# First batch of a spectral mixer: how its 64-point transforms are loaded, laid out and transposed

## The chip, the cores and the metric

The kernel runs on one core of one Trainium2 chip. The metric is the device time of one execution in microseconds, as the median of several runs. A profile of one execution goes with it: the start, the length and the waits of every instruction on each engine of the core.

The engines are named as the profile names them: PE is TensorE's matmul and PEld its weight load, DVE is VectorE, ACT is ScalarE, POOL is GpSimd, SP is SyncE, which here only issues DMAs.

## The reference

The input x has 8 batches of 3008 rows and 256 channels, all fp32. Two steps are computed.

1. A global filter: a real Fourier transform along the 3008 rows, a product with a complex filter, and the inverse transform.
2. An MLP-mixer layer on the result y: a token MLP across the rows (3008 to 256, ReLU, 256 to 3008) with a residual, then a channel MLP (256 to 1536, ReLU, 1536 to 256) with a residual.

```python
y = irfft(rfft(x, axis=1) * (filt_r + 1j * filt_i), n=3008, axis=1)
h = np.maximum(y.transpose(0, 2, 1) @ w_tok1, 0.0) @ w_tok2
u = y + h.transpose(0, 2, 1)
out = u + np.maximum(u @ w_ch1, 0.0) @ w_ch2
```

The mixer's weights arrive as 8-byte floating-point numbers; the kernel turns them into fp32 on the chip.

## The kernel before

**The transform.** 3008 is 47 x 64. The kernel does the transform of 3008 in two stages: first transforms of length 64 (over n2), with rows n1 and 47 - n1 laid together in one tile of 128 partitions, and then transforms of length 47 (over n1), one for each of 32 frequencies k2. Between them the data have to change places: what was a row index in the free dimension has to become a partition. For the batches after the first this goes through DRAM (`z_tmp`). For the first batch, which nothing can overlap with, it is done on the chip by DVE's transposition of 32 x 32 blocks.

**The first batch, step by step.** The constants at the top are A = 24 (rows n1 in a half), XC = 2, NXC = 12, K2 = 32, D = 256, P = 128 and HALF = 64.

- `x_load` (L486) loads one of 12 units. For batch 0 a unit is 4 rows n1 and 128 of the 256 channels (`xc, dc = 2 * XC, D // 2`, L489): units 0 to 5 hold the left half of the channels, 6 to 11 the right half. A piece that lies together in DRAM is 128 fp32 (512 bytes). The lower 64 partitions are loaded by SP, the upper 64 by POOL. The last unit of each half has a missing row and takes two small DMAs more on POOL (L512 and L513).
- `a_unit` (L528) is a matmul of the unit (128 x 512) with the table `wa0`, and for batch 0 a copy by ACT (L533) into the buffer `turned`. Two PSUM banks are used in turn.
- `turned` (L211 to L213) is [128, 32, 256], with the row index s (24 used, 8 zeroed by a memset at L1235) outside and the channel d inside. Its tile also holds `wa0` at its end.
- After unit 5 and again after unit 11, DVE turns the channels that are complete, 16 at a time (L617 to L621). Each of the 16 instructions takes 16 channels x 32 rows s in place, with a step of 256 fp32 between successive s.
- `b_unit(k)` (L640), for the 32 values of k, is a matmul (L642) whose moving operand is `turned[:, k, :]`, 256 fp32 that lie together, and a product with the filter on DVE (L647). `bi_unit(k)` (L650) is the inverse of that stage: four matmuls (L656), a copy on ACT (L666) and, for each pair of k, a store to `g_tmp`.

**What lies beside it.** While `b_unit` and `bi_unit` run, the same loop (L1240 to L1269) turns the token MLP's weights into fp32 in 16 steps, one for each pair of k: loads by SP or POOL, ACT L276, DVE L278 to L284, PE L322 and L323, ACT L325. The filter of each pair of k is loaded by POOL (`filt_load`, L236 to L243), copied to the upper partitions by ACT (`filt_double`, L248), and its table is turned by ACT (L255 and L256).

**The order of the work.** The schedule is manual: instructions are issued on each engine in the order in which the program text produces them. The generator `dft(GROUPS[0])` gives up control after each unit, and the loop at L1240 places other work there. At `i == NXC - 1`, which is after the last unit and before the second group of transpositions, it issues on ACT the copies of the first weight tiles (`copies()`) and the loads of four constants of 128 x 128 (L1251): `wa`, `was`, `wai` and `ident`. `ident` is used by the last six of the weight conversions on PE, the others from the second batch's transform and the first mixing step on.

**After the first batch** the result is read back from `g_tmp` (L778), the token sums run on PE (L784), and then the mixer runs through 8 batches of 6 blocks of rows and 6 blocks of channels, with the transforms of the following batches set between its steps. This takes the rest of the time.

Of the kernel before, what the change touches and what calls it, by code (L numbers as in the profile page):

```python
# [10 lines left out]
FP32 = mybir.dt.float32  # L11
# [11 lines left out]
D = 256  # L23
P = 128
K2 = 32
A = 24
KR = 4 * A
KH = KR // 2
HALF = 64
XC = 2  # L30
NXC = A // XC
# [5 lines left out]
WC = 2  # L37
# [14 lines left out]
AP = A // 2  # L52
W1S = 7
IN_B = 16
EARLY = 12
GROUPS = ((0,), (1, 2), (3, 4), (5, 6), (7,))

# [70 lines left out]
def kernel(  # L128
# [11 lines left out]
    nc = tc.nc  # L140
# [69 lines left out]

    turned = wcp.tile([P, K2 * D + P], FP32, tag="wc", name="turned")  # L211
    wa0 = turned[:, K2 * D:]
    turned = turned[:, 0:K2 * D].rearrange("p (s d) -> p s d", d=D)  # L213
    chan = []


# [233 lines left out]
    def copies():  # L450

        while copied[0] < len(tiles) and copied[0] <= ended[0] + 1:
            advance(copy)
            copied[0] += 1
# [34 lines left out]
    def x_load(b, c, i, queue=None):  # L489

        where, tag = ((t3p, "t3"), (tp, "t"), (vp, "v"), (up, "u"), (t1p, "t1"), (t2p, "t2"), (wbp, "wb"))[c // 2 if b == 0 else 6]
        xc, dc = (2 * XC, D // 2) if b == 0 else (XC, D)
        d0, c = divmod(c, A // xc)
        j = i - XB
        if b and j >= 0:
            j %= XF
            t = filts[j // 2][:, j % 2]
        else:
            t = where.tile([P, xc, dc], FP32, tag=tag, name="x")

        def rows(n1, ap):
            xb = x[b]
            return bass.AP(tensor=xb.tensor, offset=xb.offset + n1 * D + d0 * dc, ap=ap + [[1, dc]])

        for h in range(2):
            n = xc - 1 if h and (c + 1) * xc == A else xc
            q = queue or (nc.gpsimd if b == 0 and h else nc.sync)
            q.dma_start(t[h * HALF:(h + 1) * HALF, 0:n, :],
                        rows(A + c * xc if h else A - 1 - c * xc, [[N1 * D, N2], [D if h else -D, n]]))
            if n < xc:  # L510

                q.dma_start(t[HALF:P - 1, n, :], rows(N1, [[N1 * D, N2 - 1]]))  # L512
                q.dma_start(t[P - 1:P, n, :], rows(0, [[N1 * D, 1]]))  # L513
        xs[b, c + d0 * (A // xc)] = t

    def rows_of(t_d, b):
        g, i = place_of[b]
# [10 lines left out]
    def a_unit(b, c):  # L528
        ps = bank(free_bank())
        nc.tensor.matmul(ps, wa0 if b == 0 else wa, xs.pop((b, c)).rearrange("p a d -> p (a d)"), start=True, stop=True)  # L530
        if b == 0:
            d0, c = divmod(c, NXC // 2)
            nc.scalar.copy(out=turned[:, ts(c, 2 * XC), ds(d0 * P, P)], in_=ps.rearrange("p (a d) -> p a d", d=P))  # L533
            return
        z_out(b, ps, c, nc.scalar)

# [20 lines left out]
    def dft(bs):  # L557
# [44 lines left out]
        for i, u in enumerate(todo):  # L602
            if tiled:
                now, sd = sd, x_sums(*todo[i + 1], i + 1) if i + 1 < len(todo) else None
                more(1)
                a_pair(*u, now)
                yield "a" if i + 1 < len(todo) else "w"
                continue
            if first and i in (0, 2):
                w_load(i // 2)  # L610
            if first and i in (6, 8):
                table_load(i // 2 - 1)
            a_unit(*u)
            if bs != GROUPS[1] or i >= XB:
                more(1)
            yield "a" if i + 1 < len(todo) else "w"
            if first and (i + 1) % (NXC // 2) == 0:  # L617

                for d in range(i // (NXC // 2) * P, (i + 1) // (NXC // 2) * P, 16):
                    v = turned.rearrange("p s d -> p d s")[:, d:d + 16, :]  # L620
                    nc.vector.transpose(v, v)  # L621
        t2s, t3s, prods = {}, {}, {}
        wide = per * nb

# [14 lines left out]

        def b_unit(k):  # L640
            ps = bank("pg").rearrange("p (b d) -> p b d", b=2)[:, 0:nb, :]
            nc.tensor.matmul(ps, wbs[k // WC][:, 0:2 * P:2, k % WC], turned[:, k, :].unsqueeze(1), start=True, stop=True)  # L642
            t = filts_0[k // KC % len(filts_0)]
            if k == 0:
                prods["all"] = p1p.tile([P, 2, 2, D], FP32, tag="p1", name="p1")
            p1 = prods["all"][:, k % 2]
            nc.vector.tensor_tensor(out=p1, in0=ps.to_broadcast([P, 2, D]), in1=t[:, :, k % KC, :], op=ALU.mult)  # L647
            prods[k] = (p1[:, 0:1], p1[:, 1:2])
# [583 lines left out]

    with tc.manual_schedule():
        nc.sync.dma_start(wa0, wa0_d)
        nc.vector.memset(turned[:, A:K2, :], 0.0)  # L1235
        for t in filts:
            nc.vector.memset(t, 0.0)
        half = 0
        second = dft(GROUPS[1])
        for i, _ in enumerate(dft(GROUPS[0])):  # L1240
            if i == 0:
                nc.scalar.dma_start(wai_t, wait_d)
            k = i - NXC - 2

            if i < NXC:
                if i in (1, 3, 5, 7, 9):
                    start()
                if i == NXC - 1:
                    copies()
                    for t, src in ((wa, wa_d), (was, was_d), (wai, wai_d), (ident, ident_d)):  # L1250
                        nc.scalar.dma_start(t, src)  # L1251
            elif k >= 0:
                if k == K2 - 5:
                    pause.append(True)
                while half < 2 * IN_B * (k + 1) // K2:
                    if half % 2:
                        convert_end()
                    else:
                        convert_middle()
                    half += 1  # L1260

                if 19 <= k < 25:
                    t4_load(0, k - 19, 0, PARTS[1])
                elif 26 <= k < 29:
                    for c in range(2):
                        t4_load(0, 2 * (k - 26) + c, PARTS[1], PARTS[2])
                elif k in (30, 31):
                    for c in range(3):
                        t4_load(0, 3 * (k - 30) + c, PARTS[2], PARTS[3])  # L1269
        pause.clear()  # L1270

        fill(5)
        for c in range(A // TC4):
            t4_load(0, c, PARTS[3], P, (nc.sync, nc.gpsimd)[c % 2])
        both = wcp.tile([P, 2, JP, 7, P], FP32, tag="wc", name="wc")

        chan.extend((both[:, 0], both[:, 1]))
        next(second)
        for i in range(IN_B, A // 2 + TC * W2G):
            convert()  # L1280
            if i == A // 2 + BY_PE - 1:
                sum_up()
                acc = token_sums(0)

        ahead[0](XF, nc.gpsimd)
        h1s[0] = token_relu(0, acc)
        for dh in range(DH):
            convert()
            u_part(0, 0, dh)
        for f in v_steps(0, 0):  # L1290
            f()
        convert_end(False)
        for _ in range(XB):
            next(second)
        group, todo, done = -1, iter(()), True

        def next_ready(b):
            return done or b != GROUPS[group][-1]

        coming = "a"
        n = MT * JP
        for b, i, place in mix(next_ready):
            if group + 1 < len(GROUPS) and b == GROUPS[group + 1][0]:
                if not done:
                    raise AssertionError("the filter's steps don't fit beside the mixer's")
                group += 1
                done = group + 1 == len(GROUPS)
                todo = iter(()) if done else dft(GROUPS[group + 1]) if group else second  # L1310
                coming = "a"
            if done:
                continue
            jp = i % JP
            if coming in "aw":
                due = place == 1 or (place != 1.5 if group == 0 else coming == "w")
            elif group:
                tail = i >= n - JP
                due = (jp, place) in {"b": ((1, 1.5), (3 if tail else 4, 1.5)), "m": ((2, 2) if tail else (3, 1), (5, 1)),
                                      "i": ((0, 1.5), (3 if tail else 4, 1.5))}[coming]  # L1320
            else:
                due = (jp - (coming == "i")) % JP in ((5, 1, 2, 3) if i < 4 * JP else (5, 0, 1, 2, 3)) and place == {"b": 1, "m": 2, "i": 0}[coming]
            if coming == "a" and group == 0 and i < JP - 1:
                due = {0: 2, 1: 0, 1.5: 0, 2: 1}[place]
            for _ in range(due):
                if not done:
                    coming = next(todo, "end")
                    done = coming == "end"
# [30 lines left out]
```

## Time and profile before

| What | Value |
|---|---|
| Time, median of 3 runs | 2419.13 us (2417.92 to 2422.47) |
| The profiled execution's own time | 2419.85 us |
| Span of its instructions | 2418.1 us |
| PE busy | 2378.0 us, 98% of the span |
| DVE busy | 1940.6 us, 80% |
| First L642 matmul | 31.44 us after the span's start |
| First token-sum matmul (L784) | 111.56 us |
| Mean granted TensorE clock | 0.995 of full speed |

A row of a group of instructions reads: line, engine, operation, output and inputs by their names in the program, shapes, count, then busy time in us and the mean length of one in ns, and then the idle time of the engine just before them with what ended it. A row in order of time begins with start and length in us. Where several instructions are merged into one row (x16), the length is that of the whole group. The length of one instruction is longer than the distance from one start to the next, because instructions of an engine overlap a little.

### The profile page before, as it was taken

To read this page: it belongs to the slowest core of one execution; us is meant where nothing else is said; L and a number is where in the kernel's file an instruction comes from. 1 tells how busy PE (TensorE), PEld (TensorE's weight loads), DVE (VectorE), ACT (ScalarE), POOL (GpSimd) and SP (SyncE) were. 2 spreads that over 40 slices of the span, in tenths; PEclk is the share of its full clock that TensorE was granted. 3 is DMA by queue.
4 is the path that set the end of the run, shared out by engine and by line. 5 is a ranking of instruction groups with operands and counts; after the bars stand their busy time and mean duration, and the time that the engine had idled before them with its cause. 6 is when DMAs were issued, how large, how long until landed. Compare 5 with 4: busy or idle time off the path is not lost.

```text
span 2418.1 us, 35463 instructions
## 1 busy us (share of the span) xinstructions
PE 2378.0 (98%) x12340; PEld 1987.3 (82%) x12340; DVE 1940.6 (80%) x3673; ACT 685.9 (28%) x1339; POOL 619.8 (26%) x1115
## 2 busy tenths in 40 slices
PE   7999999999999999999999999999999999999998
PEld 4666676978888888987888888897888988898887
DVE  7798778787887888777888888877888777777776
ACT  5733322232221222123222222313222222222222
POOL 7476332113111211211121112112212112112121
PEclk8999999999999999999999999999999999999999
DMA  9985546554343232545344223434434111311100
GB/s 211 254 233 168 156 143 177 158 158 135 111 132 95 79 89 72 168 125 156 101 121 136 79 78 86 123 122 127 125 109 143 58 60 36 115 63 31 40 14 21
DMA packets 186011, 278.65 MB, mean 115 GB/s; under 512 B 35101, under 2 KB 122859, under 8 KB 185832
## 3 DMA queue, kind: packets, MB, share of 16 engines
q1 hardware_dynamic: 139544, 212.56, 29.3%
q0 software_dynamic: 34688, 53.83, 8.4%
q10 hardware_dynamic: 11600, 10.00, 1.3%
q8 instruction: 98, 1.61, 0.3%
q14 instruction: 81, 0.66, 0.1%
HBM read 193.52 MB, written 82.72 MB: 114 GB/s over the span
## 4 chain that ended last, share of the span: by engine, by line
PE 88%; DVE 6%; DMA 3%; issue 1%; ACT 1%; SPq 0%; POOL 0%; DVEq 0%; ACTq 0%; POOLq 0%
PE ps_po L1003 33%; PE ps_pg L969 18%; PE ps_pg L985 14%; PE ps_b L523 4%; PE ps_b L835 3%; PE ps_acc L890 3%; PE ps_acc L835 2%; PE ps_b L890 2%; PE ps_b L868 2%; PE ps_acc L868 2%; PE ps_pg L523 1%; DVE t L947 1%; DMA filt<-in_x_dram 1%; PE ps_b L784 1%; DVE hh L947 1%
## 5 line engine op out<-in xcount | busy, mean ns | idle before, releaser
L1011 POOL DMA_DIRECT2D out_dram<-r x752 | 408.7, 552 | 1539.2 <-issue 933.8
L990 ACT ACTIVATE hh<-hh 128x512 f32<-128x512 f32 (+1 forms) x576 | 347.7, 621 | 994.3 <-DVE hh L947 985.7
L947 DVE TENSOR_TENSOR hh<-ps_pg,s 128x512 f32<-128x512 f32 (+3 forms) x864 | 481.8, 585 | 178.8 <-ACT s L972 176.6
L1003 PE MATMUL ps_po<-t,wc 128*128 128x256 f32 (+1 forms) x2296 | 549.6, 379 | 1.8 <-DVE t L947 1.8
L1003 PEld LDWEIGHTS ps_po<-t,wc 128*128 128x128 f32 x2296 | 427.1, 190 | 119.7 <-issue 37.7
L969 PE MATMUL ps_pg<-v,wc 128*128 128x256 f32 (+1 forms) x1728 | 414.4, 376 | 0.1
L1003 PE MATMUL ps_po<-hh,wc 128*128 128x256 f32 (+1 forms) x1722 | 412.0, 375 | 0.7 <-POOL wc L382 0.7
L969 PEld LDWEIGHTS ps_pg<-v,wc 128*128 128x128 f32 x1728 | 328.1, 190 | 40.5 <-DVE v L947 3.2
L1003 PEld LDWEIGHTS ps_po<-hh,wc 128*128 128x128 f32 x1722 | 326.9, 190 | 39.3 <-POOL wc L382 1.9
L985 PE MATMUL ps_pg<-u,wc 128*128 128x256 f32 (+1 forms) x1152 | 292.9, 377 | 1.3 <-DVE hh L947 1.3
L947 DVE TENSOR_TENSOR t<-t,hh 128x256 f32<-128x256 f32 (+1 forms) x576 | 245.5, 426 | 19.8
L985 PEld LDWEIGHTS ps_pg<-u,wc 128*128 128x128 f32 x1152 | 216.8, 190 | 44.3 <-DVE hh L947 13.8
L947 DVE TENSOR_TENSOR s<-ps_pg,hh 128x512 f32<-128x512 f32 (+1 forms) x288 | 196.0, 681 | 30.3 <-DVE hh L947 0.5
L972 ACT COPY s<-ps_pg 128x256 f32<-128x256 f32 (+1 forms) x288 | 106.0, 368 | 350.8 <-PE ps_pg L969 348.6
L947 DVE TENSOR_TENSOR t<-hh 128x512 f32<-128x512 f32 (+1 forms) x288 | 195.3, 678 | 0.6 <-ACT hh L990 0.6
L969 PE MATMUL ps_pg<-u,wc 128*128 128x256 f32 (+1 forms) x576 | 169.6, 376 | 2.5 <-DVE hh L947 2.5
L985 PE MATMUL ps_pg<-v,wc 128*128 128x256 f32 (+1 forms) x576 | 168.7, 375 | 0.0
L947 DVE TENSOR_TENSOR u<-ps_acc,u 128x256 f32<-128x256 f32 (+1 forms) x84 | 46.2, 550 | 97.4 <-PE ps_acc L890 66.7
L969 PEld LDWEIGHTS ps_pg<-u,wc 128*128 128x128 f32 x576 | 108.1, 190 | 18.8 <-DVE hh L947 5.7
L985 PEld LDWEIGHTS ps_pg<-v,wc 128*128 128x128 f32 x576 | 109.1, 190 | 12.6
L947 DVE TENSOR_TENSOR u<-ps_b,u 128x512 f32<-128x512 f32 (+2 forms) x126 | 74.5, 591 | 28.9 <-PE ps_b L890 26.7
L890 PE MATMUL ps_acc<-w 128*128 128x256 f32 (+1 forms) x336 | 85.5, 377 | 1.0 <-ACT t L539 1.0
(161 smaller groups left out, 2655.3 us busy)
## 6 DMA issues: line engine op xcount, KB each, us to landing
w<-w_tmp SPq DMA_DIRECT2D x84, 448.0 KB
w<-w_tmp SPq DMA_DIRECT2D x35, 896.0 KB
out_dram<-r POOLq DMA_DIRECT2D x696, 32.0 KB, 2.9
g_tmp<-t SPq DMA_DIRECT2D x112, 192.0 KB
t<-g_tmp SPq DMA_DIRECT2D x42, 512.0 KB
t<-z_tmp SPq DMA_DIRECT2D x180, 96.0 KB
z_tmp<-t SPq DMA_DIRECT2D x60, 256.0 KB
filt<-in_x_dram SPq DMA_DIRECT2D x90, 128.0 KB
```

The lines of the kernel that those rows point to most:

```text
L523: nc.tensor.matmul(outs(i, j), stat(i, j), mov(i, j), start=True, stop=True)
L784: nc.tensor.matmul(acc[:, t, :], w1[:, a, ts(t, P)], t4[b, a // TC4][:, a % TC4, :], start=(a == 0 and t == 0), stop=(a == A - 1 and t == ...
L835: nc.tensor.matmul(ps[:, at], w[:, n], mov, start=(j == 0 and i in (0, 2)), stop=(j == AP - 1 and i >= 5))
L868: nc.tensor.matmul(ps[:, ds(q * P, n)], t4[b, c][:, r, ts(dh, P)], wai[:, 0:n], start=(first and q == 0), stop=(not first and q == 3))
L890: nc.tensor.matmul(ps[:, ds(j * hw, hw)], h1[:, n, :], w2m[m % 2][:, at, 0:hw], start=(i < 2 and j == 0), stop=(j == len(todo) - 1))
L947: nc.vector.tensor_tensor(out=out, in0=in0, in1=in1, op=op)
L969: nc.tensor.matmul(ps[:, 0:hw], chan[0][:, jp, n, :], mov, start=True, stop=True)
L972: nc.scalar.copy(out=s[:, 0], in_=g[0][:, 0, 0:hw])
L985: nc.tensor.matmul(ps[:, 0:hw], chan[0][:, jp, n, :], mov, start=True, stop=True)
L990: nc.scalar.activation(out=hs, in_=hs, func=AF.Relu)
L1003: nc.tensor.matmul(po[i][:, j, 0:hw], chan[1][:, jp, n, :], mov, start=(jp == 0 and first == 1), stop=(jp == JP - 1 and last == 1))
L1011: q.dma_start(bass.AP(tensor=ob.tensor, offset=ob.offset + row * D + g * cw, ap=[[N1 * D, 32], [D if h else -D, n], [1, cw]]), blocks[ts(g ...
```

## The change

It has four parts, all in the first batch's path.

1. A unit is now 2 rows n1 and all 256 channels, so that a piece that lies together in DRAM is 256 fp32 (1 KB). There are still 12 units, with one missing row in all, so the small POOL DMAs come once and not twice.
2. `turned` is laid out as [128, 64, 32, 4]: the channel d is split into q (64) and r (4), and the row index s stands between them. Successive s are 4 fp32 (16 bytes) apart, and successive q are 128 fp32 apart. ACT's copy writes runs of 8 fp32 from runs of 4 in PSUM. The moving operand of `b_unit` is 64 runs of 4 fp32.
3. All 16 transpositions come after the last unit. Each takes 16 values of q, the 32 rows s and one value of r.
4. The loads of the four constants go from ACT, where they stood ahead of the first filter copy, to SP at the fifth step of the next stage (k == 4).

```diff
+TR = 4
-    turned = turned[:, 0:K2 * D].rearrange("p (s d) -> p s d", d=D)
+    turned = turned[:, 0:K2 * D].rearrange("p (q s r) -> p q s r", s=K2, r=TR)
...
-        xc, dc = (2 * XC, D // 2) if b == 0 else (XC, D)
-        d0, c = divmod(c, A // xc)
+        xc = XC
...
-            t = where.tile([P, xc, dc], FP32, tag=tag, name="x")
+            t = where.tile([P, xc, D], FP32, tag=tag, name="x")
...
         if b == 0:
-            d0, c = divmod(c, NXC // 2)
-            nc.scalar.copy(out=turned[:, ts(c, 2 * XC), ds(d0 * P, P)], in_=ps.rearrange("p (a d) -> p a d", d=P))
+            nc.scalar.copy(out=turned[:, :, ts(c, XC), :], in_=ps.rearrange("p (a q r) -> p q a r", q=D // TR, r=TR))
...
-            if first and (i + 1) % (NXC // 2) == 0:
-
-                for d in range(i // (NXC // 2) * P, (i + 1) // (NXC // 2) * P, 16):
-                    v = turned.rearrange("p s d -> p d s")[:, d:d + 16, :]
-                    nc.vector.transpose(v, v)
+            if first and i + 1 == NXC:
+                for d in range(0, D, HALF):
+                    for r in range(TR):
+                        v = turned[:, d // TR:(d + HALF) // TR, :, r]
+                        nc.vector.transpose(v, v)
...
-            nc.tensor.matmul(ps, wbs[k // WC][:, 0:2 * P:2, k % WC], turned[:, k, :].unsqueeze(1), start=True, stop=True)
+            nc.tensor.matmul(ps.rearrange("p b (q r) -> p (b q) r", r=TR), wbs[k // WC][:, 0:2 * P:2, k % WC],
+                             turned[:, :, k, :], start=True, stop=True)
...
-        nc.vector.memset(turned[:, A:K2, :], 0.0)
+        nc.vector.memset(turned[:, :, A:K2, :], 0.0)
...
                 if i == NXC - 1:
                     copies()
+            elif k >= 0:
+                if k == 4:
                     for t, src in ((wa, wa_d), (was, was_d), (wai, wai_d), (ident, ident_d)):
-                        nc.scalar.dma_start(t, src)
-            elif k >= 0:
+                        nc.sync.dma_start(t, src)
```

More of the change, by code (lines that the diff above doesn't have):

```diff
@@ L498, in x_load @@
         else:
-            t = where.tile([P, xc, dc], FP32, tag=tag, name="x")
+            t = where.tile([P, xc, D], FP32, tag=tag, name="x")
         def rows(n1, ap):
             xb = x[b]
-            return bass.AP(tensor=xb.tensor, offset=xb.offset + n1 * D + d0 * dc, ap=ap + [[1, dc]])
+            return bass.AP(tensor=xb.tensor, offset=xb.offset + n1 * D, ap=ap + [[1, D]])
         for h in range(2):
@@ L513, in x_load @@
                 q.dma_start(t[P - 1:P, n, :], rows(0, [[N1 * D, 1]]))
-        xs[b, c + d0 * (A // xc)] = t
+        xs[b, c] = t
     def rows_of(t_d, b):
```

## The prediction

> **What bounds the kernel now.** I read the page first, then the order of time from 0 to 250 us, then a table of windows, last the groups with shapes kept apart.
>
> ```profile
> span 2418.1 us, 35463 instructions
> PE 2378.0 (98%) x12340; PEld 1987.3 (82%) x12340; DVE 1940.6 (80%) x3673; ACT 685.9 (28%) x1339; POOL 619.8 (26%) x1115
> ```
>
> TensorE (PE) is busy for 98% of the span. The edit leaves the number of its matmuls alone, so the question is when PE can start its long run. The order of time, cut to the lines that matter (start, length, engine, line, what, and in brackets the idle time before and what ended it):
>
> ```profile
> 20.10 1.10 PE L530 MATMUL ps_acc<-x,turned 128*128 128x512 f32 x2 [1.39 <-DMA x<-in_x_dram]
> 21.24 0.59 ACT L533 COPY turned<-ps_acc 128x512 f32<-128x512 f32 x1 [1.90 <-PE ps_acc L530]
> 14.15 17.19 DVE L621 STREAM_TRANSPOSE turned<-turned 128x512 f32<-128x512 f32 x16 [7.94 <-ACT turned L533]
> 26.93 0.68 ACT L276 ACTIVATE both<-st 128x512 f32<-128x512 f32 x1 [4.53 <-DMA st<-in_moe_w_tok_dram]
> 29.09 1.05 ACT L248 COPY filt<-filt 64x1024 f32<-64x1024 f32 x1 [1.48 <-DMA filt<-in_filt_r_dram]
> 31.44 2.07 PE L642 MATMUL ps_pg<-turned,wb 128*128 128x256 f32 x4 [10.24 <-issue]
> ```
>
> The twelfth length-64 unit is transformed at 20.10 us and copied out by 21.83 us. VectorE (DVE) transposes without a gap from 14.15 to 31.34 us: eight transpositions run while the second half of the units is still loading, eight more behind them. PE then starts the next stage (L642) 0.1 us later. The profile calls that wait "issue", but the end of the DVE row gives it away. Is PE the limit from there on?
>
> ```profile
> 2.00:20.00 18.00, 13.27 (x22) 4.25 (x22) 9.58 (x10) 6.46 (x12) 12.98 (x25) 1.00 1.07 228
> 31.40:39.30 7.90, 7.86 (x19) 5.08 (x20) 5.08 (x9) 3.44 (x6) 6.91 (x14) 0.63 1.06 216
> 39.30:56.70 17.40, 17.40 (x65) 13.11 (x64) 13.14 (x24) 14.94 (x27) 13.26 (x25) 1.00 0.91 227
> 56.70:74.10 17.40, 17.40 (x65) 13.12 (x64) 13.29 (x24) 15.54 (x28) 12.52 (x23) 1.00 0.98 248
> 74.10:91.50 17.40, 17.40 (x65) 13.16 (x64) 13.05 (x25) 15.49 (x29) 12.17 (x22) 1.00 0.92 232
> ```
>
> Columns: window, PE, PEld, DVE, ACT, POOL busy with counts, clock, DMA share, GB/s. In three windows of four pairs each PE is busy for all 17.40 us with the same 65 matmuls: 4.35 us a pair. So PE limits this stage, and a later start moves it as a whole. From 91.5 to 188 us the limit passes to the copies on ACT and DVE, the reload of g, the token sums on PE and DVE's conversions. All of them follow the stage in program order, so a delay passes through at a factor of about 1. The price of the change is thus the new time of L642's start less 31.44 us.
>
> [...]
>
> ```profile
> L621 DVE STREAM_TRANSPOSE turned<-turned 128x512 f32<-128x512 f32 x16 | 17.2, 1158 | 7.9 <-ACT turned L533 7.9
> L1082 DVE STREAM_TRANSPOSE r<-u 128x512 f32<-128x512 f32 x80 | 52.3, 686 | 0.0
> L255 ACT COPY turn_i<-wb 64x192 f32<-64x192 f32 x16 | 8.6, 539 | 0.4
> L248 ACT COPY filt<-filt 64x1024 f32<-64x1024 f32 x16 | 16.7, 1044 | 1.8 <-DMA filt<-in_filt_r_dram 1.5
> L656 PEld LDWEIGHTS ps_b<-p,wb 128*96 128x96 f32 x32 | 7.6, 261 | 1.0 <-DVE p L647 0.9
> L656 PEld LDWEIGHTS ps_b<-p,turn_i 128*96 128x96 f32 x32 | 5.5, 170 | 1.0
> ```
>
> A transposition of the same 128x512 takes 686 ns from dense rows (L1082) and 1158 ns at steps of 1 KB (L621; 17.19/16 = 1.074 us start to start). ACT reads at 16-byte steps in L255: 192 elements in 539 ns. The L248 and L990 rows (1024 elements 1044 ns, 512 elements 630 ns) give 0.81 ns an element and 216 ns fixed; so L255 pays (539-216)/192 = 1.68 ns, twice the dense price. PE's weight load pays 261 ns for 96 columns at 16-byte steps against 170 dense. [...] L1082 against L1051 (128 elements, 278 ns) gives (686-278)/384 = 1.06 ns an element, L621 about twice that. [...]
>
> **The change part by part.** *Loads of whole rows.* The same 3.08 MB in half as many packets, and POOL issues two fewer DMAs before the last unit (one L512 and L513 pair, 0.58 + 0.54 us). The x data take 3.08 MB / 228 GB/s = 13.5 us of a saturated queue; [...] Bounds: 0 (other loads take the room) and 3.5 (3.08 MB at the 271 GB/s of the window from 24 to 26 us, 11.4 us, and the issues on top). I take 2.0.
>
> *Copies into the new layout.* Twelve copies of 586 ns; PSUM is now read, and SBUF written, in 16- and 32-byte pieces. Bounds 0.54 (a little quicker) and 1.1 us (double). Only the last one lies on the path; I take 0.6, no difference. The first memset (1.76 us, done at 3.0) has four microseconds of cover; doubled it would still end before the first copy at 7.25, having pushed the three filter memsets to 8 us.
>
> *Transpositions.* Still 16 of 128x512. Their elements stand 16 bytes apart instead of 1 KB[...]. Bounds: 0.60 us (dense, 686 ns less the 0.08 us by which L621's length exceeds its spacing) and 1.2; I take 1.074. All now wait for the last copy, so the eight that had run beside the loads (8 x 1.074 = 8.6 us) come onto the path. Before, 0.9 us of them lay on it already: the second eight were ready at 21.83 but started at 22.74.
>
> *Sum at L642.* Last copy at 21.83 - 2.0 = 19.83; plus 16 x 1.074 = 17.19 and 0.05 hand-over: 37.07 us, against 31.34. Delay 5.7 us.
>
> *Moving operand of L642.* 32 units x 2 matmuls now read runs of four fp32. [...] I take 0. Bounds: 0 (it already runs at 0.215 us for 256 columns, the dense pace) and one extra column time for each run, 0.215/4 = 0.054 us x 64 = +3.4 us in a stage where PE is the limit.
>
> *Constants.* Four ACT issues (0.34 + 0.44 + 0.44 + 0.45 us, 26.96 to 28.74) vanish ahead of L248. ACT ends that work at 31.27 now and would at about 29.5; DVE ends at 37, so it is worth 0. On SP four issues of about 0.4 us stand between a pair of table loads and the token-weight load that follows at the fifth unit of the stage. SP issues some 2.5 us per 4.35-us pair, so 1.85 us is free each pair and the 1.7 us fits; both loads run pairs ahead. Without that cover it would cost 1.7 us once. The constants are needed from 89.95 us (ident) and 140 us (wa) on. The 256 KB are moved, not saved.
>
> Sum against the profiled execution (2419.85 us, span 2418.1): 2419.85 + 5.7 = 2425.6. That execution is 0.72 above the median of 2419.13, so the median becomes **2424.8 us**, 0.24% slower. About 0.2% (4.84 us) is what a measurement of this kernel tells from no change.
>
> **Rivals.**
> 1. *Not slower: the step of 16 bytes is fast on DVE.* Speaking for it: no DVE instruction of before has that step; the 1 KB step might be the special one. Against: ACT and PE pay double at 16 bytes. Price: 16 x 0.60 = 9.6, L642 at 19.83 + 9.65 = 29.5, next late is ACT at 29.5; 1.9 us earlier: 2417.2. It decides below (31.34 - 19.83)/16 = 0.72 us a transposition.
> 2. *The load hides more of it:* x 3.5 us earlier, plus 0.6 us of the 2.1 us that PE waits for the reload of g at 109.4: 5.73 - 1.5 - 0.6 = 3.6, 2422.7. For: that wait is a DMA's, and the queues get ahead while DVE transposes. Against: the g reload follows the stage's own writes.
> 3. *PE pays for the short runs:* 5.7 + 3.4: 2428.2. [...]
>
> **Chances.** Forecast 0.61 (own range 2423.3 to 2426.8, as x gains 3.5 to 0), rival 1 0.14, rival 2 0.13, rival 3 0.10, something else 0.02. Of the forecast some 0.52 lies above 2423.97 (0.2%); with rival 3 and the rest 0.64 slower. Same: 0.09 + 0.13 + most of rival 1 = 0.33. Faster by 4.84 us needs L642 at 26.6, that is 0.42 us a transposition, below the dense row: 0.03. The range takes the forecast's own, rival 2, most of rival 3 and the upper edge of rival 1: 2418.0 to 2429.0, leaving out about 0.17.
>
> **What would show it.** L621's successor: 16 back to back, spacing near 1.07 us, starting near 19.9; L642's first near 37.1; pairs still 4.35 us; the first matmul of the token sums near 117.2 (111.56 now); the last L530 near 18. Wrong if the spacing is under 0.8 us, if pairs stretch, or if the shift at L642 isn't found again at 188 us.

## The result, and the profile after

The changed kernel takes 2428.75 us in the median of 8 runs (2424.63 to 2430.24), against 2421.12 us (2417.92 to 2422.47, 8 runs) of the kernel before beside it. The ratio is 1.0034, with a 95% interval of 1.0025 to 1.0043: 0.34% slower, 6 to 10 us. The prediction had the sign, but 0.24%: 2424.8 us against a median of 2419.13, or 5.7 us. The profiled execution took 2429.18 us. Its page begins:

```profile
span 2427.4 us, 35461 instructions
PE 2378.4 (98%) x12340; PEld 1990.0 (82%) x12340; DVE 1940.1 (80%) x3673; ACT 685.8 (28%) x1339; POOL 617.2 (25%) x1113
```

The span is 9.3 us longer, and PE's busy time 0.4 us: the loss is waiting. The order of time of the kernel after, around the transpositions (start, length, engine, line, what, and the idle time before with what ended it):

```profile
18.77 0.58 ACT L532 COPY turned<-ps_acc 128x512 f32<-128x512 f32 x1 [0.36 <-PE ps_acc L530]
19.39 15.54 DVE L620 STREAM_TRANSPOSE turned<-turned 128x512 f32<-128x512 f32 x16 [13.17 <-ACT turned L532]
25.41 0.67 ACT L277 ACTIVATE both<-st 128x512 f32<-128x512 f32 x1 [4.73 <-DMA st<-in_moe_w_tok_dram]
26.11 1.04 ACT L249 COPY filt<-filt 64x1024 f32<-64x1024 f32 x1
35.03 2.07 PE L641 MATMUL ps_pg<-turned,wb 128*128 128x256 f32 x4 [16.30 <-issue]
```

The last copy ends at 19.35 us (21.83 before), all sixteen transpositions follow it, and PE's first matmul of the next stage starts at 35.03 (31.44 before): 3.6 us late, less than the 5.7 predicted. The filter's copy on ACT, 3 us earlier, waits for nobody. In the table of windows (PE, PEld, DVE, ACT, POOL busy with counts, clock, DMA share, GB/s) stand the other two surprises:

```profile
2.00:20.00 18.00, 13.66 (x24) 4.89 (x24) 4.34 (x5) 7.03 (x13) 14.79 (x31) 1.00 1.01 241
31.40:39.30 7.90, 4.27 (x9) 2.88 (x10) 6.42 (x10) 0.14 (x1) 1.26 (x4) 0.50 0.79 166
39.30:56.70 17.40, 17.40 (x61) 12.68 (x60) 12.46 (x22) 14.87 (x27) 12.82 (x24) 0.94 0.52 134
56.70:74.10 17.40, 17.40 (x66) 13.11 (x66) 13.37 (x25) 15.47 (x29) 14.12 (x26) 1.00 0.92 228
74.10:91.50 17.40, 16.91 (x62) 12.41 (x62) 12.00 (x22) 14.15 (x26) 12.19 (x22) 1.00 1.06 272
```

From 39.3 to 56.7 us the DMA engines are busy for a share of 0.52, where it was 0.91. Later, from 74.1 to 91.5, they are at 1.06 and PE no longer fills the window. The groups with shapes kept apart:

```profile
L620 DVE STREAM_TRANSPOSE turned<-turned 128x512 f32<-128x512 f32 x16 | 15.5, 1093 | 13.2 <-ACT turned L532 13.2
L1082 DVE STREAM_TRANSPOSE r<-u 128x512 f32<-128x512 f32 x80 | 52.3, 687 | 0.0
L249 ACT COPY filt<-filt 64x1024 f32<-64x1024 f32 x16 | 16.7, 1043 | 0.4
L641 PE MATMUL ps_pg<-turned,wb 128*128 128x256 f32 x64 | 21.1, 416 | 16.3 <-issue 16.3
```

A transposition takes 15.54/16 = 0.971 us, 10% less than before (1.074 by the same division) and far from the 0.60 put for dense rows (L1082). L641 takes 416 ns, as before: here PE pays nothing for runs of four. Read along the order of time, the delay grows: 3.6 us at L641, 6.45 us at the first token-sum matmul (118.01 against 111.56), 9.07 us at the second group of L876 matmuls (199.20 against 190.13), and 9.3 us at the end. So there is a second loss inside the stage and a third after it.

**The second loss.** SP's own queue in the kernel after, 31 to 63 us:

```profile
31.34 1.91 SPq L344 DMA_DIRECT2D st<-in_moe_w_tok_dram  x2
40.89 4.43 SPq L575 DMA_DIRECT2D wb<-wbi_t  x2
45.37 1.27 SPq L344 DMA_DIRECT2D st<-in_moe_w_tok_dram  x2
46.74 5.76 SPq L575 DMA_DIRECT2D wb<-wbi_t  x2
52.54 0.59 SPq L1253 DMA_DIRECT2D wa<-wa_t  x1
53.18 0.43 SPq L1253 DMA_DIRECT2D was<-was_t  x1
53.65 0.51 SPq L1253 DMA_DIRECT2D wai<-wai_t  x1
55.01 0.32 SPq L1253 DMA_DIRECT2D ident<-ident_t  x1
55.43 1.28 SPq L344 DMA_DIRECT2D st<-in_moe_w_tok_dram  x2
```

and of the kernel before, from 31 to 45 us:

```profile
31.12 1.09 SPq L576 DMA_DIRECT2D wb<-wbi_t  x2
32.26 1.27 SPq L343 DMA_DIRECT2D st<-in_moe_w_tok_dram  x2
33.64 1.17 SPq L576 DMA_DIRECT2D wb<-wbi_t  x2
34.85 1.35 SPq L343 DMA_DIRECT2D st<-in_moe_w_tok_dram  x2
37.30 1.66 SPq L576 DMA_DIRECT2D wb<-wbi_t  x2
44.03 1.27 SPq L343 DMA_DIRECT2D st<-in_moe_w_tok_dram  x2
```

A row of two loads that is 4.43 or 5.76 us long has a wait inside it. Before, SP issued ten loads between 31 and 39 us; after, it issued two and then stood until 40.89 us, because the buffers it fills come free only as PE uses them. SP's own waits name that release (us in total, times, longest):

```profile
SPq L575 <- PE ps_acc L656: 8.6, 3, 7.6
```

The constants stand behind those waits and hold SP from 52.54 to 55.33 us, 2.8 us. My estimate of free time in SP's row had left the waits out. At the end of the stage PE waits for converted token weights (1.6 us for DVE L285, 1.5 us for ACT L277); in the kernel before it waits there for the reload of g, 2.1 us.

**The third loss.** What PE waits for in the first mixing step, from the waits of the kernel after,

```profile
PE ps_pg L969 <- POOL wc L382: 3.3, 1, 3.3
PE ps_pg L969 <- DVE hh L947: 2.6, 4, 0.9
```

and from those of the kernel before:

```profile
PE ps_pg L969 <- DVE hh L947: 2.5, 3, 1.3
```

PE now waits 3.3 us once for a converted weight tile from POOL. But not all of it is lost. In the kernel before the token sums took 22.64 us, here 20.96: there the granted clock (the share of its full speed that PE was given) fell to 0.50 for a part of that stretch (0.92 in the mean), here it stayed at 1.00. (The 0.94 from 39.3 to 56.7 us in the table is no such dip. In both kernels PE starts the stage at a granted clock of 0.50, for 5.8 us before and 6.4 us after, and with the later start a part of that falls into this window.) PE thus made up 1.7 us on its way to POOL's conversion, and the wait is worth 3.3 - 1.7 = 1.6 us. Nor does the wait come with the change alone: e2 and e4 below start on time, take 20.96 us for the token sums, and wait 2.4 us at the same place.

The path between the two profiled executions: 3.6 (start), 2.9 (stage, 6.45 - 3.59), 1.6 (POOL less the clock), 1.0 not assigned up to the second L876, 0.2 after it: 9.3 us.

### The profile page after: what moved, and what is told of

Its sections match the earlier page's. It is cut to its first block, busy times and chain, and to the rows that moved or that the text cites. A ratio compares the mean times of both kernels' runs of the same rounds, so it can differ in the third digit from the quotient of the medians.

```text
span 2427.4 us, 35461 instructions
## 1 busy us (share of the span) xinstructions
PE 2378.4 (98%) x12340; PEld 1990.0 (82%) x12340; DVE 1940.1 (80%) x3673; ACT 685.8 (28%) x1339; POOL 617.2 (25%) x1113
## 4 chain that ended last, share of the span: by engine, by line
PE 85%; DVE 6%; DMA 2%; issue 1%; ACT 1%; POOL 1%; SPq 0%; DVEq 0%; ACTq 0%; POOLq 0%
PE ps_po L1003 33%; PE ps_pg L969 18%; PE ps_pg L985 14%; PE ps_b L523 4%; PE ps_b L835 3%; PE ps_acc L890 3%; PE ps_acc L835 2%; PE ps_b L890 2%; PE ps_acc L868 2%; PE ps_b L868 2%; PE ps_pg L523 1%; DVE t L947 1%; DVE hh L947 1%; DMA filt<-in_x_dram 1%; DVE s L947 1%
```

## The experiments

Three theories went in. Theory 1: the late start costs what it is late, and the constants on SP cost the rest. Theory 2: the late start alone is amplified. The third, formed from the first four runs: the DMA queues are nearly full in this stage (a DMA share of 0.91 to 1.06 in the kernel before, from 31.4 to 91.5 us), and time in which they idle isn't made up. The runs fall into four groups, e1 to e4, e5 to e9, e10 to e13 and e14 to e17, each measured on a chip of its own. All ratios stand against runs of the kernel before on the same chip (medians 2419.97, 2420.43, 2419.82 and 2419.80 us for the four groups).

| Run | Edit | Median us | Ratio (95%) | First L641/L642 |
|---|---|---|---|---|
| e1 | after, constants on ACT | 2425.69 | 1.0023 (1.0014 to 1.0032) | 35.90 |
| e2 | before, constants on SP | 2421.90 | 1.0007 (0.9999 to 1.0015) | 30.45 |
| e3 | before, runs of 4 by halves | 2418.51 | 0.9995 (0.9987 to 1.0003) | 29.79 |
| e4 | before, transpositions issued at the end | 2419.67 | 1.0000 (0.9992 to 1.0008) | 31.36 |
| e5 | before, runs of 2 by halves | 2418.17 | 0.9989 (0.9981 to 0.9997) | 25.61 |
| e7 | before, whole rows alone | 2426.73 | 1.0028 (1.0019 to 1.0037) | 35.84 |
| e8 | after, runs of 2, constants on ACT | 2419.16 | 0.9994 (0.9986 to 1.0002) | 29.70 |
| e9 | after, constants on POOL | 2425.47 | 1.0021 (1.0014 to 1.0029) | 35.52 |
| e10 | after again | 2429.29 | 1.0038 (1.0026 to 1.0051) | 35.01 |
| e11 | after, constants twice | 2432.36 | 1.0053 (1.0041 to 1.0066) | 35.46 |
| e12 | after, constants later on SP | 2426.09 | 1.0031 (1.0018 to 1.0043) | 34.72 |
| e13 | e5 with constants on POOL | 2421.70 | 1.0009 (1.0001 to 1.0017) | 25.90 |
| e14 | e1 with four tiny loads on SP | 2425.72 | 1.0022 (1.0014 to 1.0030) | 34.91 |
| e15 | before, last transposition 4 times more | 2424.82 | 1.0022 (1.0014 to 1.0031) | 35.63 |
| e16 | e1 again | 2425.95 | 1.0023 (1.0013 to 1.0033) | 35.08 |
| e17 | before, last transposition 8 times more | 2430.92 | 1.0043 (1.0030 to 1.0057) | 40.61 |

### One part at a time (e1 to e4)

e1, the changed kernel with the constants where they were:

```diff
                 if i == NXC - 1:
                     copies()
+                    for t, src in ((wa, wa_d), (was, was_d), (wai, wai_d), (ident, ident_d)):
+                        nc.scalar.dma_start(t, src)
             elif k >= 0:
-                if k == 4:
-                    for t, src in ((wa, wa_d), (was, was_d), (wai, wai_d), (ident, ident_d)):
-                        nc.sync.dma_start(t, src)
```

> The changed kernel with one part undone: the four constants are loaded by ACT at their old place. Theory 1 (the constants on SP cost a second loss): the stage starts at 35.0 us as in the changed kernel, 3.6 us late, SP keeps its pace, and only those 3.6 us reach the end: ratio to before 1.0015. Theory 2 (the late start itself brings the second loss, wherever the constants are): as the changed kernel, 1.0034.

e2 is the opposite edit, the constants' move alone in the kernel before.

> The kernel before with this part alone: the four constants go to SP at the fifth step of the stage. The stage starts at 31.4 us in both theories. Theory 1: SP falls behind, the store copies on ACT wait, about 4 us are lost: ratio 1.0016. Theory 2: nothing is lost: 1.0000.

e3 keeps the half units and the transpositions after each half, with the new kind of layout (`turned`, its memset and the matmul are written as in the changed kernel):

```diff
+TR = 4
...
+            nc.scalar.copy(out=turned[:, ts(d0, P // TR), ts(c, 2 * XC), :],
+                           in_=ps.rearrange("p (a q r) -> p q a r", q=P // TR, r=TR))
...
+                for d in range(i // (NXC // 2) * P, (i + 1) // (NXC // 2) * P, 16 * TR):
+                    for r in range(TR):
+                        v = turned[:, d // TR:d // TR + 16, :, r]
+                        nc.vector.transpose(v, v)
```

> The kernel before with the new layout alone (runs of four channels), still half-width units and transpositions after each half. Both theories: a transposition takes 0.97 us start to start instead of 1.07, the second eight start at 21.9 and end at 29.7, the stage starts 1.6 us earlier: ratio 0.9993. If an earlier start upsets or helps the DMA queues as Theory 2 has it for a later one, the gain is about double: 0.9987.

e4 only issues the sixteen transpositions of the kernel before after the last unit:

```diff
-            if first and (i + 1) % (NXC // 2) == 0:
+            if first and i + 1 == NXC:
...
-                for d in range(i // (NXC // 2) * P, (i + 1) // (NXC // 2) * P, 16):
+                for d in range(0, D, 16):
```

> The kernel before with one part alone: all 16 transpositions after the last unit, at the old step of 1 KB and with the old loads. The stage starts at 21.83 + 17.2 = 39.1 us, 7.7 us late. Theory 1: these 7.7 us reach the end and no more: ratio 1.0032. Theory 2: the loss doubles on the way (3.6 us became 7.6 in the changed kernel): 1.0060 or more.

With the constants off SP the loss falls from 1.0034 to 1.0023 (e1), between the two expectations, and it does not vanish. The move alone gives 1.0007 (e2), also between the two, with an interval that touches no change. The layout by halves is on the quicker side of no change (e3), as expected, with an interval that includes it. e4 missed what both theories expected. The order of time of e4 says why:

```profile
14.04 17.21 DVE L621 STREAM_TRANSPOSE turned<-turned 128x512 f32<-128x512 f32 x16 [7.83 <-ACT turned L533]
31.36 2.06 PE L642 MATMUL ps_pg<-turned,wb 128*128 128x256 f32 x4 [10.85 <-issue]
```

The first eight still start at 14.04 us. The last unit's place in the program holds nothing back on DVE, which has no other work there; a transposition waits only for the copies of the channels it reads. So "all at the end" is not what costs. The whole-row units are: every channel then needs all twelve.

### What a step costs, and the late start (e5, e7, e8)

e7 is e1 with the old layout: whole rows, steps of 1 KB, constants on ACT.

> Whole-row units and all sixteen transpositions behind the last one, but the old layout (steps of 1 KB) and the constants on ACT as before: the late start alone. The last copy ends at 19.4 and sixteen transpositions at 1.07 us end at 36.6, so L642 starts at 36.6 (5.2 us later than before). Theory 1 (a late start passes through at a factor of 1): ratio 1.0021. Theory 3 (the DMA queues are a second limit of the stage, so time in which they idle is not made up, and POOL's late conversion adds a wait near 149 us): the loss at the first conversion's end is 6.5 to 7, ratio 1.0026 to 1.0030, with the DMA share from 39.3 to 56.7 us at 0.6 or less against 0.91.

e5 is e3 and e8 is e1, both with a step of 8 bytes between successive rows (each transposition still takes 16 values of q):

```diff
-TR = 4
+TR = 2
```

> The kernel before with the new kind of layout, but with runs of two channels (successive rows 8 bytes apart), units of half the channels and the transpositions after each half, constants on ACT as before. Theory A ([...] it runs near the dense price): spacing of 0.60 to 0.70 us, the second eight end near 26.8, L642 then starts near 29.1 when ACT's filter copy ends, ratio 0.9988 to 0.9992. Theory B (any step costs the same): spacing 0.97, L642 at 29.8 as in the run with runs of four by halves, ratio 0.9993 to 0.9997. If PE pays for runs of two in L642, a pair takes more than 4.35 us, and the sum is 1.4 us or more later per 0.022 us of each matmul; expected in neither.

> The changed kernel with runs of two channels in place of four (8-byte steps) and the constants on ACT as before. Theory A (dense price at 8 bytes): sixteen transpositions at 0.60 to 0.70 us from 19.4 end at 29.0 to 30.6, L642 starts at about 30, and the kernel is not slower: ratio 0.9990 to 1.0000, with no late DMA. Theory B (any step costs 0.97): L642 at 35 and ratio 1.0023 as in the run with the constants back on ACT.

The transpositions in e7:

```profile
18.68 17.06 DVE L618 STREAM_TRANSPOSE turned<-turned 128x512 f32<-128x512 f32 x16 [12.47 <-ACT turned L531]
```

and in e8, with PE's start:

```profile
19.99 9.61 DVE L620 STREAM_TRANSPOSE turned<-turned 128x512 f32<-128x512 f32 x16 [13.78 <-ACT turned L532]
29.70 2.06 PE L641 MATMUL ps_pg<-turned,wb 128*128 128x256 f32 x4 [10.37 <-DVE turned L620]
```

One instruction of 128x512 takes 17.06/16 = 1.066 us at 1 KB, 0.971 at 16 bytes and 9.61/16 = 0.601 at 8 bytes. That is the spacing that Theory A of these runs named, 0.60 to 0.70 us, and 0.60 is what I had put for dense rows. Why 8 bytes are that quick and 16 are not, no run here shows. PE pays almost nothing for runs of two: 37.24 to 41.61 in e8, 4.37 us a pair against 4.35.

e8 has whole rows and all sixteen transpositions behind the last copy, like the changed kernel, and is not slower (0.9994). So the late start of L641, 35 us instead of 30, is the cause of the loss that e1 keeps. e7 is as late and loses as e1 does, or a little more. Its ratio of 1.0028 and its DMA share of 0.58 from 39.3 to 56.7 us are what the third theory had asked for, but the interval includes the 1.0021 of Theory 1.

e5 beats both kernels (0.9989, 2.3 us between the medians), as expected, but far less than its start promises. PE's second pair there waits for ACT's filter copy. ACT in e5:

```profile
25.92 0.67 ACT L277 ACTIVATE both<-st 128x512 f32<-128x512 f32 x1 [4.58 <-DMA st<-in_moe_w_tok_dram]
25.94 0.34 ACTq L1255 DMA_DIRECT2D wa<-wa_t  x1
26.32 0.44 ACTq L1255 DMA_DIRECT2D was<-was_t  x1
26.80 0.45 ACTq L1255 DMA_DIRECT2D wai<-wai_t  x1
27.28 0.46 ACTq L1255 DMA_DIRECT2D ident<-ident_t  x1
28.09 1.04 ACT L249 COPY filt<-filt 64x1024 f32<-64x1024 f32 x1 [1.50 <-DMA filt<-in_filt_r_dram]
```

### An earlier start (e13)

e13 is e5 with the four constants moved out of that place, to POOL at k == 4.

> The kernel before with runs of two channels by halves (the run at 0.9989) and besides the constants on POOL at the fifth step, so that ACT no longer issues them ahead of the first filter copy. After the quicker transpositions that copy is what PE's second pair waits for (it stands at 31.7 where the first stands at 25.6). Theory: ACT is 1.7 us earlier there, so the second pair starts at about 30, and the ratio falls to 0.9980 to 0.9984. Rival (the filter's own load is what the copy waits for, or the stage is bound by its DMAs afterwards): ratio stays at 0.9988 to 0.9991.

The first half of the theory held in part: the second pair starts at 30.91 us, 0.8 earlier than in e5 where 1.7 was expected, and PE's next L645 matmul after it at 34.67 us, 2.0 earlier than in e5 and 4.6 earlier than before. The ratio went the other way, to 1.0009. The waits of PE in e13 show where the gain went:

```profile
PE ps_b L788 <- DMA t<-g_tmp: 5.5, 1, 5.5
```

The token sums wait 5.5 us for the reload of g, where they waited 2.1 us before (2.9 in e5). They start at 110.47, 1.1 us before those of the kernel before, though PE's last L645 matmul of the stage starts 4.4 us ahead of the kernel before (96.20 against 100.59). An early start is thus in good part taken back by the reload; why the run ends up slower than e5, and not level, isn't shown. The two were measured on different chips, and their profiled executions took the same time (2420.12 and 2420.03 us), so the traces cannot tell.

### The constants (e9 to e12, e14, e16)

e9 moves the constants of the changed kernel from SP to POOL, at the same step:

```diff
                 if k == 4:
                     for t, src in ((wa, wa_d), (was, was_d), (wai, wai_d), (ident, ident_d)):
-                        nc.sync.dma_start(t, src)
+                        nc.gpsimd.dma_start(t, src)
```

> The changed kernel with the four constants loaded at the same point of the program (fifth step of the stage) but by POOL instead of SP. Theory 1a (they cost time because they stand in SP's row, behind its waits and ahead of its next loads): the loss falls to that of the run with the constants back on ACT, ratio 1.0023. Theory 1b (they cost time because their 256 KB take room in a stage whose DMA engines are nearly full): ratio stays at 1.0032 to 1.0036.

e10 repeats the changed kernel:

> The changed kernel once more, on the same chip as the three runs beside it, so that the constants on SP can be set against it directly. Expected: ratio 1.0030 to 1.0036 in every theory. If it came out at 1.0025 or less, the difference to the runs with the constants on ACT (1.0023) or POOL (1.0021) would be noise between chips.

e11 doubles the dose (each `dma_start` twice):

> The changed kernel with each of the four constants loaded twice by SP at the fifth step: a double dose (eight DMAs, 512 KB in that place). Theory S (SP's row of issues and waits is what they delay, in a stretch in which SP is already late): another 2.5 to 4 us, ratio 1.0044 to 1.0052. Theory N (the loads cost nothing and the loss is all from the late start): ratio as of the changed kernel, 1.0032 to 1.0036. If only the bytes counted, 256 KB at about 250 GB/s would be 1.0 us, ratio 1.0038.

e12 puts them at `k == 20`:

> The changed kernel with the constants on SP at the twenty-first step of the stage (k == 20, about 79 us) instead of the fifth (about 44 us). Theory S1 (they hurt because SP is behind in the first twenty microseconds after the late start and has caught up later): the loss falls to that of the runs without them on SP, 1.0021 to 1.0024. Theory S2 (SP has no slack anywhere in the stage): ratio stays at 1.0032 or more.

e14 is e1 with four loads of one row on SP at k == 4; their data are those that already stand there:

```diff
             elif k >= 0:
+                if k == 4:
+                    for t, src in ((wa, wa_d), (was, was_d), (wai, wai_d), (ident, ident_d)):
+                        nc.sync.dma_start(t[0:1], src[0:1])
```

> The changed kernel with the constants back on ACT, and at the fifth step four loads of 512 bytes each on SP (one row of each constant again). Theory S (the four issues and their place in SP's row cost, not the bytes): 2.5 to 3.5 us more than the repeat of the kernel without them beside it, as if the whole constants stood there. Rival (the 256 KB cost): no difference to that repeat, within 0.0005 of its ratio.

e16 repeats e1 beside it:

> The changed kernel with the constants back on ACT once more, for comparison on the same chip. Expected 1.0021 to 1.0025 in every theory.

With the constants on SP the two measurements give 1.0034 and 1.0038; without them on SP four give 1.0021 to 1.0023. The difference is 0.0012 to 0.0016, some 3 to 4 us. No group of runs measured both, and singly the intervals overlap (1.0025 to 1.0043 against 1.0014 to 1.0032), so a difference between chips is not excluded, though the four without agree on three chips. On one chip stands only the second dose: e11 against e10 costs 3.1 us more between the medians (0.0015 of the ratio, 3.6 us), close to what Theory S expected, and no run of the one reaches into the other's. Part of that may be e11's own: each second load stands behind the first to the same place (SP waits 2.1 us for the first load of `wai` and 1.8 us for that of `ident`), and SP reaches its next token-weight load at 63.20 us, 8.7 us later than in e10. The two simple explanations both fall. Four issues as such cost nothing (e14: 1.0022, e16: 1.0023, on one chip), so my Theory S in its plain form is wrong. The bytes as such cost nothing either, when POOL loads them (e9). What is left is the bytes in SP's row. SP in e9, with nothing between table loads and token-weight loads:

```profile
47.29 5.14 SPq L575 DMA_DIRECT2D wb<-wbi_t  x2
52.52 1.30 SPq L344 DMA_DIRECT2D st<-in_moe_w_tok_dram  x2
```

There the token-weight load that follows goes out at 52.52 us, in the changed kernel at 55.43. That SP's later loads then come late as a whole fits the stalls of PE after 82 us, but which transfer delays which was not traced to the end. From the first L641 to the token sums the changed kernel takes 83.0 us, e10 82.5 and e11 86.8, and no other trace more than e17's 82.0, except the early e5 and e13. That agrees, but it proves little: a dip of the granted clock lies inside this stretch in some traces (e1 and e10, a mean of 0.91 from 91.5 to 109.5 us, worth 0.09 x 18 = 1.6 us) and not in others (after and e17, 1.00 there). e12 lies between (1.0031 by the ratio, 2426.09 by the median) and tells nothing apart.

### The late start alone (e15, e17)

The kernel before, with DVE turning the last sixteen channels four (e17: eight) times more:

```diff
                     v = turned.rearrange("p s d -> p d s")[:, d:d + 16, :]
-                    nc.vector.transpose(v, v)
+                    for _ in range(5 if d == D - 16 else 1):
+                        nc.vector.transpose(v, v)
```

> The kernel before with the last transposition repeated four more times (twice turns it back), 4 x 1.074 = 4.3 us of delay on DVE ahead of the first L642, and nothing else changed. Theory 1 (a late start passes at a factor of 1): +4.3 us, ratio 1.0018. Theory 2 (it is amplified by 1.3 or more, as POOL's first conversion comes late as well): +5.6 us or more, ratio 1.0023 or more, with a wait of PE for POOL at L969 that the kernel before does not have. Theory 4 (a second limit, the reload of g, gives part of it back): +3 us or less.

> The kernel before with the last transposition repeated eight more times, 8.6 us of delay. Theory 1: +8.6 us, ratio 1.0036. Theory 2: +11 us or more, ratio 1.0046 or more. If a fixed wait comes with any delay, rather than a factor, the second 4.3 us cost 4.3 us after the first have cost more.

e15's start is at 35.63 us, as late as the changed kernel's, with the loads, the layout and the constants of before. The delay itself came out longer than expected, as the rows of the transpositions in e15 and e17 show:

```profile
13.44 22.08 DVE L622 STREAM_TRANSPOSE turned<-turned 128x512 f32<-128x512 f32 x20 [7.23 <-ACT turned L533]
13.51 27.00 DVE L622 STREAM_TRANSPOSE turned<-turned 128x512 f32<-128x512 f32 x24 [7.30 <-ACT turned L533]
```

The sixteen of before take 17.19 us, so the four repeats add 4.9 us and the eight 9.8, about 1.22 us each and not 1.074. e15 costs 5.0 us between the medians (3.4 to 7.5 by the interval of the ratio) for these 4.9, and e17 11.1 us (7.3 to 13.8) for 9.8. That is a factor of 1.0 to 1.1, as Theory 1 has it. Theory 2's factor of 1.3 isn't seen, nor the part that Theory 4 has given back, nor the jump with any delay that was allowed for in e17, and the profile of e15 has no wait for POOL. Over all the runs the wait for POOL goes with the token sums' length: where they take 22.6 to 22.9 us (before, e5, e13, e15, e16) it is at most 0.2 us; where they take 20.9 to 21.0 it is 0.7 to 3.3.

The emptied queues are seen in e15 as well. Its window from 39.3 to 56.7 us:

```profile
39.30:56.70 17.40, 17.40 (x63) 12.98 (x63) 13.18 (x24) 15.34 (x27) 13.11 (x24) 0.98 0.64 161
```

The DMA share is 0.64 there, 0.91 before. So the late start by itself lets the queues run empty, as the loads wait for buffers that PE has yet to use (SP's table loads wait 15.4 us in five waits for PE's L657, from 31 to 120 us; 7.1 us in four for the same matmul, L656, before). Whether that idle time must be paid, as the third theory has it, these executions leave open. From its start to the token sums e15 takes 115.13 - 35.63 = 79.5 us and e7 79.6, no more than the 80.1 of before; e1 takes 81.6 and e17 82.0.

## Why the prediction was right and wrong

- **The direction and its reason were right.** The transpositions come onto PE's path, PE starts late, and nothing later gives it back. e8 shows it by taking the lateness away, e15 by adding the lateness alone.
- **Loads (2.0 us, my estimate, on a range of 0 to 3.5; the numbers given for the upper end make 3.3).** The pair of traces says 2.5. But the start of the last copy spreads: 19.6 to 21.2 us in eight executions with half units, 18.1 to 19.6 in ten with whole rows, with means of 20.3 and 18.9. The gain is about 1.4 us, and the trace of before was the latest of its eight. "Half as many packets" was not seen on POOL's queue: it moved 835 packets in the first 20 us before and 880 after, SP's 3914 and 2541. What a packet costs, no run isolates.
- **Copies (0.6 us, no difference).** Right: 585 ns.
- **Transpositions (16 x 1.074).** All sixteen did stand behind the last copy; the term was too large, 0.971 each, which is 1.6 us of the sum. That a step of 16 bytes costs what one of 1 KB costs was my estimate; it was close: 0.971 against 1.066.
- **Sum at L642 (37.07, a delay of 5.7).** 35.03, a delay of 3.6 in the pair of traces. (The sum sets L642's new start against the old end of DVE, 31.34; against L642's old start, 31.44, it is 0.1 us less.) The mean of eight executions of the changed kernel and its variants with that layout is 35.2, and the three with the old transpositions (before, e2, e4) start at 30.5 to 31.4: some 4 us.
- **Moving operand (0, my estimate; rival 3 had up to 3.4 us).** Right: 416 ns, and pairs of 4.35 us up to 82 us.
- **Constants (0).** This is the step that failed. "SP issues some 2.5 us per 4.35-us pair, so 1.85 us is free" counted the issues of SP and not its waits. The fallback, "it would cost 1.7 us once", was too small as well: e1, e9, e14 and e16 against the changed kernel and e10 put it at 3 to 4 us, across groups of runs, and the second dose in e11 at 3.1 to 3.6 us on one chip.
- **Carry ("a factor of about 1").** Right: 1.0 to 1.1 in e15 and e17. The whole-row kernels without the constants on SP (e1, e9, e14, e16) lose 5.0 to 6.2 us between the medians for a start some 4 us late; the intervals include 4, and what the rest is, if it is real, stays open.
- **Together:** 4 to 5 us for the start and 3 to 4 for the constants make the 8 to 9 us measured (0.34% and 0.38%). That the forecast came as near as 5.7 us is in part luck: a start term that was too high by about 1.6 us hid part of the constants' cost.
- **Rivals.** Rival 1's price (16 x 0.60) is what e8 runs at, with steps of 8 bytes. At 16 bytes it was wrong, and its point of decision, 0.72 us, lies between the two. The reason against it ("ACT and PE pay double at 16 bytes") held for ACT by the estimate from L255 (1.68 ns an element against 0.81); PE's weight load took 261 ns against 170, 1.5 times as long. Rival 2 was right in part: the queues did get ahead while DVE transposed, only to stand empty afterwards. Rival 3 was wrong: PE did not pay.

Open remain why the constants need both their bytes and SP's row to cost, which wait carries that cost to PE, and why e13 is slower than e5.

## What to carry to other kernels

Work that waits for the last piece of a load lies on the path (e7, 1.0028), and where it is issued does not decide that (e4, 1.0000); ask which pieces each step needs before making pieces larger. A queue's free time is what is left after its waits, in the schedule as it will be and not as it was. And when a strided step can't be avoided, try the smallest change of layout that makes the step shorter still: here a transposition took 0.601 us at 8 bytes and 0.971 at 16, and the 8 bytes moved the start of the stage by some 5 us, though little of that reached the end (0.9989 in e5, 1.0009 in e13). Last, read an inserted delay from its own trace before dividing by it.

## What the runs showed of the hardware

- A DVE transposition of 128x512 fp32 took 0.601 us at steps of 8 bytes (e8), 0.971 at 16 bytes (after) and 1.066 at 1 KB (e7), each as a sixteenth of its group. Of the three steps, most of the difference lies between 8 and 16 bytes.
- The same transposition repeated on its own output took about 1.22 us more for each repeat (e15, e17), where sixteen on different channels took 1.07 each.
- PE's granted clock was 0.50 when the stage started, in the kernel before (from 31.44 us) and in the changed kernel (from 35.03). It was 1.00 again after 5.8 us before and after 6.4 in the changed kernel. In every trace the first four matmuls of the stage took 2.06 or 2.07 us together. A later dip to 0.50 came in some executions and not in others: with one the token sums of the kernel before took 22.64 us (0.92 in the mean), without one those of the changed kernel 20.96 (1.00).
- A PE matmul with 256 moving columns in runs of four or two fp32 took what it took with 256 in a row: 416 ns in the changed kernel and in e8, 416 in the kernel before (e7, also with 256 in a row, 408).
- SP's loads were released by the end of stores that ACT had issued to another tensor (`SPq L344 <- DMA g_tmp<-t`, 9.9 us in four waits from 31 to 120 us of the changed kernel). The trace names the releaser; it does not say why a load should wait for it.
